# One core, XCiT attention into a gelu layer: hand-written issue order, fp32 batch-0 loads, transposed scores, two-bank gelu

## Chip, core and metric

The kernel runs on one core of a Trainium2 chip. The metric is device time in microseconds (us) of one execution. Before the change three timed runs gave 914.63, 913.44 and 914.12 us.

## What is computed

For each of 4 batches, q, k and v are 6080 x 256 in fp32. The attention is over channels: a 256 x 256 score matrix per batch, from columns normalised over the 6080 rows. Its result goes through a 256 to 2048 to 256 layer with gelu.

```python
qn = q / (np.linalg.norm(q, axis=1, keepdims=True) + 1e-06)
kn = k / (np.linalg.norm(k, axis=1, keepdims=True) + 1e-06)
s = kn.transpose(0, 2, 1) @ qn / tau
a = softmax(s, axis=-1)
x = (v @ a).reshape(24320, 256)
h = x @ w_in
out = gelu_tanh(h) @ w_out
```

Since v @ a @ w_in = v @ (a @ w_in), both kernels make aw = a @ w_in (256 x 2048, bf16) once per batch and then need for each row of v only hp = aw.T v and yp = gelu(hp).T w_out.

## The kernel before

A batch has two stages. **The Gram stage** (L81 to L115) walks 48 tiles of 128 rows (the last has 64). Each tile has two casting loads from the POOL queue, fp32 in HBM to bf16 in SBUF (L89, L90), squares on ScalarE (q, L92) and VectorE (k, L93), two Gram matmuls of 256 columns into G (L97), and for every second tile, after an addition on VectorE (L108), one matmul with a column of ones for the sums of squares (L109). Then come the norms and the softmax: a reciprocal on one partition (L118), square roots (L120, L121), a spread over 128 partitions by small fp32 matmuls (L124, L126), the scaled scores (L138), Exp (L139), four transposes on TensorE (L147) with copies (L153), and aw in 8 pieces of 512 columns (L161), evicted by ScalarE (L167).

**The block stage** (L170 to L215) walks 12 blocks of 512 rows of v (the last has 448). v is first cast to bf16 by one DRAM to DRAM transfer per batch (L82) and read by transposing DMAs on SP (L179). Each block has 32 matmuls hp of 512 columns (L187), 16 gelu on ScalarE of 128x512 each, from one PSUM bank (L192; the pool pH has 3), 64 matmuls yp of 256 columns (L199), four copies to SBUF (L203) and one store from the ScalarE queue (L207).

Nothing in the text fixes the order between the batches: a scheduler mixes the next batch's Gram tiles with the blocks as it sees fit. Each engine then runs its own list in order. Activation functions of different table sets need a table load (ACT_TABLE_LOAD) between them; the compiler places these.

Of the kernel before, what the change touches and what calls it, by code (L numbers as in the profile page):

```python
# [12 lines left out]


@with_exitstack
def kernel(
# [16 lines left out]
    assert isinstance(tau, (int, float)), "tau expected as a trace-time scalar"
    inv_tau2 = 1.0 / float(tau) ** 2

    def ntile_rows(n0):
        return min(128, N - n0)

    n_tiles = (N + 127) // 128  # L40
# [22 lines left out]
    nc.gpsimd.tensor_copy(ident_bf, ident)
    ones_col = const.tile([128, 1], BF16)
    nc.vector.memset(ones_col, 1.0)
    ones_row = const.tile([1, 128], FP32)
    nc.vector.memset(ones_row, 1.0)

    win_st = stage.tile([128, CHUNKS, D], FP32, tag="wst")
    nc.sync.dma_start(out=win_st, in_=moe_w_in.rearrange("(c p) d -> p c d", p=128))  # L70
    win_bf = const.tile([128, CHUNKS, D], BF16)
    nc.scalar.activation(win_bf, win_st, AF.Copy)  # L72

    wout_st = stage.tile([128, FC, 256], FP32, tag="wst")
# [2 lines left out]
    nc.scalar.activation(wout_bf, wout_st, AF.Copy)

    v_bf = dram.tile([B * N, C], BF16)

    for b in range(B):  # L81
        nc.gpsimd.dma_start(out=v_bf[b * N : (b + 1) * N, :], in_=v[b])  # L82
        G = pG.tile([128, CHUNKS, 512], FP32, tag="G")
        ss = pM.tile([1, 512], FP32, tag="m")
        for it in range(n_tiles):
            n0 = it * 128
            rows = ntile_rows(n0)
            qk = qkp.tile([128, 2, 256], BF16, tag="qk")
            nc.gpsimd.dma_start(out=qk[:rows, 0, :], in_=q[b, n0 : n0 + rows, :])  # L89
            nc.gpsimd.dma_start(out=qk[:rows, 1, :], in_=k[b, n0 : n0 + rows, :])  # L90
            sq = sqp.tile([128, 512], BF16, tag="sq")
            nc.scalar.activation(sq[:rows, 0:256], qk[:rows, 0, :], AF.Square)  # L92
            nc.vector.tensor_mul(sq[:rows, 256:512], qk[:rows, 1, :],  # L93
                                 qk[:rows, 1, :])
            first, last = it == 0, it == n_tiles - 1
            for ci in range(CHUNKS):
                nc.tensor.matmul(  # L97
                    G[:, ci, 0:256],
                    lhsT=qk[:rows, 1, ci * 128 : ci * 128 + 128],
                    rhs=qk[:rows, 0, :],  # L100
                    start=first,
                    stop=last,
                )
            if it % 2 == 0 and not last:
                sq_prev = sq
            else:
                if it % 2 == 1:
                    nc.vector.tensor_add(sq_prev[:rows], sq_prev[:rows], sq[:rows])  # L108
                nc.tensor.matmul(  # L109
                    ss,  # L110
                    lhsT=ones_col,
                    rhs=sq_prev,
                    start=it <= 1,
                    stop=last,
                )  # L115

        inv = smx.tile([1, 512], FP32, tag="inv")
        nc.vector.reciprocal(inv, ss)  # L118
        rrow = smx.tile([1, 512], FP32, tag="rrow")
        nc.scalar.activation(rrow[:, 0:256], inv[:, 0:256], AF.Sqrt)  # L120
        nc.scalar.activation(rrow[:, 256:512], inv[:, 256:512], AF.Sqrt,  # L121
                             scale=inv_tau2)
        M = pM.tile([128, 512], FP32, tag="m")
        nc.tensor.matmul(M[:, 0:256], lhsT=ones_row, rhs=rrow[0:1, 0:256])  # L124
        for ci in range(CHUNKS):
            nc.tensor.matmul(M[:, 256 + ci : 257 + ci],  # L126
                             lhsT=rrow[0:1, 256 + ci * 128 : 384 + ci * 128],
                             rhs=ident[0:1, 0:1], is_transpose=True)
        rqk = smx.tile([128, 258], FP32, tag="rqk")
        nc.vector.tensor_copy(rqk, M[:, 0:258])  # L130
        rk_col = rqk[:, 256:258]

        e_bf = smx.tile([128, 2, 256], BF16, tag="ebf")
        rsum = smx.tile([128, 2], FP32, tag="rsum")
        rsinv = smx.tile([128, 2], FP32, tag="rsinv")
        for ci in range(CHUNKS):
            S = smx.tile([128, 256], FP32, tag="S")
            nc.vector.tensor_mul(S, G[:, ci, 0:256], rqk[:, 0:256])  # L138
            nc.scalar.activation(e_bf[:, ci, :], S, AF.Exp,  # L139
                                 scale=rk_col[:, ci : ci + 1],  # L140
                                 accum_out=rsum[:, ci : ci + 1])
        nc.vector.reciprocal(rsinv, rsum)

        eTp = pG.tile([128, 4, 128], BF16, tag="G")
        for ci in range(CHUNKS):
            for jc in range(CHUNKS):
                nc.tensor.matmul(eTp[:, ci * 2 + jc, :],  # L147
                                 lhsT=e_bf[:, ci, jc * 128 : jc * 128 + 128],
                                 rhs=ident_bf, is_transpose=True)
        eT = smx.tile([128, 2, 256], BF16, tag="eT")  # L150
        for jc in range(CHUNKS):
            for ci in range(CHUNKS):
                nc.vector.tensor_copy(eT[:, jc, ci * 128 : ci * 128 + 128],  # L153
                                      eTp[:, ci * 2 + jc, :])

        aw = awp.tile([128, CHUNKS, D], BF16, tag="aw")
        for ic in range(CHUNKS):
            for fs in range(D // 512):
                awps = pH.tile([128, 512], FP32, tag="h")
                for jc in range(CHUNKS):  # L160
# [6 lines left out]
                nc.scalar.activation(aw[:, ic, fs * 512 : fs * 512 + 512], awps,  # L167
                                     AF.Copy, scale=rsinv[:, ic : ic + 1])

        for blk in range(n_blocks):  # L170
# [5 lines left out]
            vT = vts.tile([128, CHUNKS, 512], BF16, tag="vT")
            r0v = b * N + t0
            for cc in range(CHUNKS):
                nc.sync.dma_start_transpose(  # L179
                    out=vT[:, cc, :cols],  # L180
                    in_=v_bf[r0v : r0v + cols, cc * 128 : cc * 128 + 128])

            gs = []
            for fc in range(FC):
                hp = pH.tile([128, 512], FP32, tag="h")
                for cc in range(CHUNKS):
                    nc.tensor.matmul(hp[:, :cols],  # L187
                                     lhsT=aw[:, cc, fc * 128 : fc * 128 + 128],
                                     rhs=vT[:, cc, :cols],
                                     start=cc == 0, stop=cc == CHUNKS - 1)  # L190
# [60 lines left out]
```

## Time and profile before

| what | value |
|---|---|
| timed runs | 913.44, 914.12 (median), 914.63 us |
| profiled execution, first to last instruction | 913.5 us |
| mean granted TensorE clock | 0.955 of 2.4 GHz |
| PE busy | 804.7 us (88%) |
| ACT busy | 503.3 us (55%) |
| DVE busy | 190.3 us (21%) |
| POOL busy | 206.5 us (23%) |

The profile gives no time of its own for the profiled execution beside its span of 913.5 us. PE is the matmul engine, PEld its weight loads, DVE VectorE, ACT ScalarE, POOL GpSimd, SP the sync engine that here issues DMAs. An engine that is called busy need not run at its peak, as matmuls are pipelined; so rates are taken from start to start.

### The profile page before, as it was taken

The numbers are of one execution on the slowest core, as the hardware profiler recorded it, in microseconds if no ns is written. First come the engines' busy times: TensorE is split into PE (matmuls) and PEld (weight loads), VectorE is DVE, ScalarE is ACT, GpSimd is POOL, SyncE is SP. The second block draws the span as 40 slices with busy tenths as digits, with TensorE's granted clock in tenths as the row PEclk, the third lists the DMA queues.
The fourth block names the chain that finished last, engine by engine and source line by source line (L and its number), as shares of the span: only waits on it lengthen the run. The fifth ranks groups of instructions, "written<-read, shape, count | busy, mean of one in ns | idle before, by whom it ended". The sixth has DMA issues, their size and how long they took to land. (4 is left out here: it accounts for less than half of the span.)

```text
span 913.5 us, 13551 instructions
## 1 busy us (share of the span) xinstructions
PE 804.7 (88%) x5136; PEld 498.9 (55%) x5184; DVE 190.3 (21%) x518; ACT 503.3 (55%) x1031; POOL 206.5 (23%) x395
## 2 busy tenths in 40 slices
PE   0537529999999979999999889999999889999998
PEld 0101206666666637575666546575757545766666
DVE  0224302121221322121212313121212210101101
ACT  0333616565656385656566485656565466465563
POOL 2649412221212232312121222312121000000000
PEclk9995659999999989999999989999999999999999
DMA  9999984353534444534444434534443102212111
GB/s 234 232 177 122 187 155 76 82 87 76 81 80 78 85 46 76 96 72 90 73 85 74 90 36 82 92 70 93 70 92 67 55 12 58 58 56 61 46 47 44
DMA packets 134624, 79.80 MB, mean 87 GB/s; under 512 B 58784, under 2 KB 133792, under 8 KB 133792
## 3 DMA queue, kind: packets, MB, share of 16 engines
q0 software_dynamic: 55360, 37.38, 30.3%
q1 hardware_dynamic: 54048, 16.66, 8.2%
q10 hardware_dynamic: 25152, 24.91, 7.9%
q8 instruction: 40, 0.66, 0.3%
q14 instruction: 24, 0.20, 0.1%
HBM read 78.91 MB, written 37.36 MB: 127 GB/s over the span
## 5 line engine op out<-in xcount | busy, mean ns | idle before, releaser
L192 ACT ACTIVATE g<-hp 128x512 bf16<-128x512 f32 (+1 forms) x768 | 384.3, 625 | 275.2 <-PE hp L187 274.7
L199 PE MATMUL yp<-wout_bf,g 128*128 128x256 bf16 (+1 forms) x3072 | 372.8, 273 | 0.1
L187 PE MATMUL hp<-vT,aw 128*128 128x512 bf16 (+1 forms) x1492 | 368.3, 377 | 3.7 <-ACT g L192 1.3
L199 PEld LDWEIGHTS <-g 128*128 128x128 bf16 (+1 forms) x3072 | 300.4, 98 | 68.8 <-issue 0.8
L187 PEld LDWEIGHTS <-aw 128*128 128x128 bf16 x1536 | 148.7, 97 | 159.9 <-issue 35.9
L89 POOL DMA_DIRECT2D qk<-in_q_dram x192 | 111.0, 578 | 449.0 <-ACT g L192 360.9
L97 PE MATMUL G<-qk 128*128 128x256 bf16 (+1 forms) x384 | 79.2, 309 | 65.6 <-DMA qk<-in_k_dram 64.7
L203 DVE COPY ysb<-yp 128x256 f32<-128x256 f32 x192 | 81.2, 423 | 257.3 <-PE yp L199 257.1
L90 POOL DMA_DIRECT2D qk<-in_k_dram x192 | 112.6, 587 | 43.2 <-DMA v_bf<-in_v_dram 39.1
L92 ACT ACTIVATE sq<-qk 128x256 bf16<-128x256 bf16 x192 | 77.0, 455 | 76.9 <-DMA qk<-in_q_dram 54.9
L93 DVE TENSOR_TENSOR sq<-qk 128x256 bf16<-128x256 bf16 x192 | 54.9, 289 | 309.1 <-DMA qk<-in_k_dram 270.5
L97 PEld LDWEIGHTS <-qk 128*128 128x128 bf16 (+1 forms) x384 | 30.5, 101 | 118.3 <-DMA qk<-in_k_dram 94.1
L108 DVE TENSOR_TENSOR sq<-sq 128x512 bf16<-128x512 bf16 x96 | 40.7, 424 | 142.3 <-ACT sq L92 137.7
L109 PE MATMUL ss<-sq,ones_col 128*1 128x512 bf16 x96 | 41.8, 448 | 11.7 <-DVE sq L108 9.9
L167 ACT ACTIVATE aw<-awps,rsinv 128x512 bf16<-128x512 f32 x32 | 19.4, 695 | 9.7 <-PE awps L161 9.7
L161 PE MATMUL awps<-win_bf,eT 128*128 128x512 bf16 x60 | 20.5, 468 | 2.9 <-DVE eT L153 2.9
L124 PE MATMUL M<-rrow,ones_row 1*128 1x256 f32 x8 | 4.9, 710 | 19.7 <-ACT rrow L120 19.7
L109 PEld LDWEIGHTS <-ones_col 128*1 128x1 bf16 x96 | 7.7, 81 | 25.1 <-issue 24.7
L72 ACT ACTIVATE win_bf<-win_st 128x4096 bf16<-128x4096 f32 x1 | 3.6, 3618 | 20.9 <-DMA win_st<-in_moe_w_in_dram 20.9
L118 DVE RECIPROCAL inv<-ss 1x512 f32<-1x512 f32 x4 | 13.4, 3346 | 3.5 <-PE ss L109 3.5
L124 PEld LDWEIGHTS M<-rrow,ones_row 1*128 1x128 f32 x8 | 2.0, 306 | 21.2 <-ACT rrow L120 21.2
L161 PEld LDWEIGHTS <-eT 128*128 128x128 bf16 x64 | 7.1, 117 | 11.3 <-issue 5.5
(27 smaller groups left out, 47.7 us busy)
## 6 DMA issues: line engine op xcount, KB each, us to landing
out_dram<-ysb ACTq DMA_DIRECT2D x44, 512.0 KB, 2.9
v_bf<-in_v_dram POOLq DMA_DIRECT2D x4, 3040.0 KB, 20.8
qk<-in_q_dram POOLq DMA_DIRECT2D x188, 64.0 KB, 2.6
qk<-in_k_dram POOLq DMA_DIRECT2D x188, 64.0 KB, 2.6
win_st<-in_moe_w_in_dram SPq DMA_DIRECT2D x1, 2048.0 KB, 22.2
wout_st<-in_moe_w_out_dram SPq DMA_DIRECT2D x1, 2048.0 KB, 13.6
vT<-v_bf SPq DMA_TRANSPOSE x96, 2.7
out_dram<-ysb ACTq DMA_DIRECT2D x4, 384.0 KB, 2.5
```

The costliest lines, as they stand in the source:

```text
L89: nc.gpsimd.dma_start(out=qk[:rows, 0, :], in_=q[b, n0 : n0 + rows, :])
L90: nc.gpsimd.dma_start(out=qk[:rows, 1, :], in_=k[b, n0 : n0 + rows, :])
L92: nc.scalar.activation(sq[:rows, 0:256], qk[:rows, 0, :], AF.Square)
L93: nc.vector.tensor_mul(sq[:rows, 256:512], qk[:rows, 1, :], qk[:rows, 1, :])
L97: nc.tensor.matmul(G[:, ci, 0:256], lhsT=qk[:rows, 1, ci * 128 : ci * 128 + 128], rhs=qk[:rows, 0, :], start=first, stop=last,)
L108: nc.vector.tensor_add(sq_prev[:rows], sq_prev[:rows], sq[:rows])
L109: nc.tensor.matmul(ss, lhsT=ones_col, rhs=sq_prev, start=it <= 1, stop=last,)
L161: nc.tensor.matmul(awps, lhsT=eT[:, jc, ic * 128 : ic * 128 + 128], rhs=win_bf[:, jc, fs * 512 : fs * 512 + 512], start=jc == 0, stop=jc = ...
L187: nc.tensor.matmul(hp[:, :cols], lhsT=aw[:, cc, fc * 128 : fc * 128 + 128], rhs=vT[:, cc, :cols], start=cc == 0, stop=cc == CHUNKS - 1)
L192: nc.scalar.activation(g[:, :cols], hp[:, :cols], AF.Gelu_apprx_tanh)
L199: nc.tensor.matmul(yp[:r, 0:256], lhsT=gs[fc][:, s * 128 : s * 128 + r], rhs=wout_bf[:, fc, :], start=fc == 0, stop=fc == FC - 1)
L203: nc.vector.tensor_copy(ysb[:r, s, :], yp[:r, 0:256])
```

## The change

The new kernel turns the scheduler off (`manual_schedule`): each engine gets its instructions in the order of the text, and generators interleave the next batch's attention with the blocks, one step behind each pair of hp tiles.

- Batch 0: q and k come in fp32 by 20 HWDGE loads from SP (9 chunks of 2 to 6 tiles, four fp32 buffers), are cast on DVE and squared on ACT chunk by chunk; the sums of squares are a 128 x 512 matmul per tile with a square of ones, so that the sums stand on all partitions. The weights are loaded after q and k and cast by DVE and POOL. v of batch 0 is cast in four pieces.
- Batches 1 to 3: casting loads from POOL of 6 tiles each; squares and an fp32 running sum on DVE; one fp32 matmul with ones at the end.
- The scores are made transposed (lhsT = q, rhs = k), so the four transposes with their copies go; the row sums of the softmax come from four small matmuls (rs). The norms come from Ln and Exp in place of reciprocal and Sqrt. aw is evicted by DVE in place of ACT.
- gelu takes 128 x 1024 from two banks, 8 per block; yp of a block is put behind the hp of the next one, 8 matmuls at a time; two yp tiles share a bank and a copy of 128x512; stores go from SP.

```diff
-    qkp = ctx.enter_context(tc.tile_pool(name="qkp", bufs=6))
+    stage = ctx.enter_context(tc.tile_pool(name="stage", bufs=4))
+    qkp = ctx.enter_context(tc.tile_pool(name="qkp", bufs=4))
...
+    pA = ctx.enter_context(tc.tile_pool(name="pA", bufs=2, space=bass.MemoryType.PSUM))
+    pH = ctx.enter_context(tc.tile_pool(name="pH", bufs=2, space=bass.MemoryType.PSUM))
     pY = ctx.enter_context(tc.tile_pool(name="pY", bufs=2, space=bass.MemoryType.PSUM))
+    ctx.enter_context(tc.manual_schedule())
...
+    def softmax_steps(b, G, sums, aw):
+        SS = sums()
+        yield
...
+            nc.vector.scalar_tensor_tensor(
+                out=junk, in0=SS[:, jc * 128 : jc * 128 + 128], scalar=1.0, in1=ident,
+                op0=ALU.mult, op1=ALU.mult, accum_out=ssc[:, jc : jc + 1])
+        nc.scalar.activation(r[:, 0:256], SS[:, 256:512], AF.Ln, bias=tiny_b)
+        nc.scalar.activation(r[:, 256:258], ssc, AF.Ln, bias=tiny_b)
+        yield
+        nc.scalar.activation(r, r, AF.Exp, scale=0.5)
+        nc.scalar.activation(r, r, AF.Ln, bias=eps_b)
+        nc.scalar.activation(r, r, AF.Exp, scale=-1.0)
+        yield
...
+            nc.scalar.activation(eT[:, jc, :], S[:, jc, :], AF.Exp,
+                                 scale=r[:, 256 + jc : 257 + jc])
+        yield
+        rs = pA.tile([128, 512], FP32, tag="a", name="rs")
...
+        nc.vector.reciprocal(rsinv, rs[:, 0:2])
+        yield
+        for fs in range(D // 512):
+            for ic in range(2):
...
+                nc.vector.tensor_scalar_mul(
+                    aw[:, ic, fs * 512 : fs * 512 + 512], ps, rsinv[:, ic : ic + 1])
+                yield
...
+    first_chunks = chunks_of([2, 5, 6, 6, 6, 6, 6, 6, 4])
...
+            nc.vector.tensor_copy(qkb[:rows, lo:hi], st[:rows, lo:hi])
+            nc.scalar.activation(sqb[:rows, lo:hi], st[:rows, lo:hi], AF.Square)
...
+        if n == 6:
+            nc.gpsimd.tensor_copy(gate[:, 0:1], st[0:1, 0, 0, 0:1])
+            nc.gpsimd.dma_start(out=v_bf[0:1024, :], in_=v[0, 0:1024, :])
...
+    for half in range(2):
+        nc.gpsimd.tensor_copy(wout_bf[:, half * 8 : half * 8 + 8, :], wout_st[half])
...
+    V_CH = [(1024, 2688), (2688, 4384), (4384, N)]
+    for lo, hi in V_CH:
+        nc.gpsimd.dma_start(out=v_bf[lo:hi, :], in_=v[0, lo:hi, :])
...
+    def attention_steps(b, aw_next):
...
+        for n in range(3):
+            load(n)
+        for _ in range(8):
+            yield
...
+                gram(G, loaded[n], s, rows, first, last)
+                flat = loaded[n][:rows, s].rearrange("p a b -> p (a b)")
...
+                    nc.vector.tensor_mul(sq[:rows], flat, flat)
+                    nc.vector.tensor_add(acc[:rows], acc[:rows], sq[:rows])
+                seen += 1
+                yield
+                if seen % 2:
+                    yield
+        def sums():
+            SS = pA.tile([128, 512], FP32, tag="a", name="SS")
+            nc.tensor.matmul(SS, lhsT=ones_f, rhs=acc)
+            return SS
+        yield from softmax_steps(b, G, sums, aw_next)
...
+            for i in range(NP):
+                hp = pH.tile([128, 2, 512], FP32, tag="h", name="hp")
...
+                nc.scalar.activation(g[:, 2 * i : 2 * i + 2, :cols], hp[:, :, :cols],
+                                     AF.Gelu_apprx_tanh)
+                if nb == 0:
+                    next(steps, None)
+                if before is not None:
+                    h = i % 2
+                    y_part(before, i // 2, h * NP, h * NP + NP)
+                next(fill, None)
```

What a generator yields takes one step of the block loop. `attention_steps` gives 8 empty steps, 72 steps for 48 Gram tiles, and 13 for the softmax and aw, of the 96 steps that 12 blocks have; so the softmax of batch b+1 falls into block 10 of batch b, and its aw into blocks 10 and 11.

**ScalarE at the softmax of a batch.** The rows of before, for a later batch; the names are the program's tiles (rrow the norms, e_bf the exponentials, g the gelu output):

```order
L120 ACT_TABLE_LOAD
L120 ACTIVATE rrow<-inv 1x256
L121 ACTIVATE rrow<-inv 1x256
L92 ACTIVATE sq<-qk 128x256 x2
L139 ACT_TABLE_LOAD
L139 ACTIVATE e_bf,rsum<-S,rqk 128x256 x2
L167 ACTIVATE aw<-awps,rsinv 128x512 x8
L192 ACT_TABLE_LOAD
L192 ACTIVATE g<-hp 128x512 x16
```

The rows of the change in block 10 of batch 0, behind a table load, the two Ln of the sums (L142, L143), a table load and one gelu:

```order
L145 ACT_TABLE_LOAD
L145 ACTIVATE r<-r 128x258
L146 ACT_TABLE_LOAD
L146 ACTIVATE r<-r,eps_b 128x258
L147 ACT_TABLE_LOAD
L147 ACTIVATE r<-r 128x258
L375 ACT_TABLE_LOAD
L375 ACTIVATE g<-hp 128x1024
L155 ACT_TABLE_LOAD
L155 ACTIVATE eT<-S,r 128x256 x2
L375 ACT_TABLE_LOAD
L375 ACTIVATE g<-hp 128x1024 x4
```

Three table loads per batch have become eight (five for batch 0, whose softmax has no gelu between its steps), and gelu stand between the steps of the softmax.

**TensorE one step later in the same block**, where the row sums rs stand between a yp group and the next hp:

```order
L319 LDWEIGHTS g
L319 MATMUL yp<-wout_bf,g 128x256
L161 LDWEIGHTS eT [waits Activation_49]
L161 MATMUL rs<-ones_bf,eT 128x1 [waits DVE_49]
L161 LDWEIGHTS eT [waits Activation_49]
L161 MATMUL rs<-ones_bf,eT 128x1
```

Before, the transposes of e_bf waited for Exp at this point; now rs does, and all hp and yp of the blocks stand behind it in the list.

**POOL at the start.** Before:

```order
L82 DMA v_bf<-in_v_dram 128x12160
masks.py:199 ISA
masks.py:199 AFFINE_SELECT ident<-ident 128x128
L89 DMA qk<-in_q_dram 128x256
L63 CAST ident_bf<-ident 128x128
L90 DMA qk<-in_k_dram 128x256
```

With the change (wst are the fp32 weights):

```order
L208 COPY gate<-st 1x1 [waits DMAHW6_49]
L209 DMA v_bf<-in_v_dram 16x16384
L247 CAST win_bf<-wst 128x2x512 [waits DMAHW4_49]
L247 CAST win_bf<-wst 128x2x512 [waits DMAHW5_49]
L250 CAST wout_bf<-wst 128x2048 [waits DMAHW6_49]
L250 CAST wout_bf<-wst 128x2048 [waits DMAHW7_49]
L258 DMA v_bf<-in_v_dram 32x13312
L258 DMA v_bf<-in_v_dram 32x13568 x2
L86 DMA qkb<-in_q_dram 128x5x256 [waits DVE_49,PE_49]
```

The rest of v and the first q and k of batch 1 are now issued behind the casts of the weights, which wait for loads that stand behind all of batch 0's q and k.

## Rows read from the trace of the kernel before

**Rows 1.** The page, part 1: busy us (share of the span), instructions.
```profile
PE 804.7 (88%) x5136; PEld 498.9 (55%) x5184; DVE 190.3 (21%) x518; ACT 503.3 (55%) x1031; POOL 206.5 (23%) x395
```

**Rows 2.** Stretches: length, busy by engine (instructions), granted clock, DMA share, GB/s.
```profile
0.00:23.00 23.00, 0.00 (x0) 0.00 (x0) 0.21 (x2) 1.36 (x2) 5.30 (x15) 1.00 0.93 234
70.00:100.00 30.00, 20.11 (x58) 4.49 (x59) 15.99 (x41) 13.33 (x31) 27.29 (x52) 0.50 1.05 128
...
724.00:742.00 18.00, 10.37 (x39) 4.30 (x39) 5.31 (x9) 11.93 (x21) 0.00 (x0) 0.81 0.02 6
...
756.00:896.00 140.00, 139.43 (x942) 92.26 (x949) 16.57 (x39) 79.23 (x158) 0.00 (x0) 1.00 0.19 53
...
120.00:124.00 4.00, 0.00 (x0) 0.00 (x0) 0.00 (x0) 0.00 (x0) 0.00 (x0) 0.50 1.10 237
```

**Rows 3.** Timeline, start of the blocks: start us, length, engine, line, count [idle <-releaser].
```profile
109.33 0.59 PE L187 MATMUL hp<-vT,aw 128*128 128x512 bf16 x2
...
130.74 0.53 POOL L90 DMA_DIRECT2D qk<-in_k_dram  x1 [13.69 <-DMA v_bf<-in_v_dram]
...
131.18 1.25 PE L97 MATMUL G<-qk 128*128 128x256 bf16 x4 [19.73 <-DMA qk<-in_k_dram]
```

**Rows 4.** Chain that ended last, blocks of batches 2 and 3: start us, length, what.
```profile
573.00 1.73 PE hp L187 x8
...
762.21 6.44 PE yp L199 x59
...
776.37 6.44 PE yp L199 x59
```

**Rows 5.** Groups by line and shape: busy us, mean ns of one | idle before, releaser.
```profile
L192 ACT ACTIVATE g<-hp 128x512 bf16<-128x512 f32 x704 | 355.3, 630 | 251.1 <-PE hp L187 250.7 <-issue 0.2
L108 DVE TENSOR_TENSOR sq<-sq 128x512 bf16<-128x512 bf16 x92 | 39.0, 424 | 128.7 <-ACT sq L92 124.2
L192 ACT ACTIVATE g<-hp 128x448 bf16<-128x448 f32 x64 | 29.0, 576 | 24.0 <-PE hp L187 24.0
L139 ACT ACT_TABLE_LOAD x4 | 5.1, 1283 | 0.1
L124 PE MATMUL M<-rrow,ones_row 1*128 1x256 f32 x8 | 4.9, 710 | 19.7 <-ACT rrow L120 19.7
L139 ACT ACTIVATE e_bf<-S,rqk 128x256 bf16<-128x256 f32 x8 | 4.0, 500 | 1.7 <-DVE S L138 1.6
L72 ACT ACTIVATE win_bf<-win_st 128x4096 bf16<-128x4096 f32 x1 | 3.6, 3618 | 20.9 <-DMA win_st<-in_moe_w_in_dram 20.9
L138 DVE TENSOR_TENSOR S<-G,rqk 128x256 f32<-128x256 f32 x8 | 3.0, 420 | 0.1
L120 ACT ACTIVATE rrow<-inv 1x256 f32<-1x256 f32 x4 | 1.7, 415 | 2.6 <-DVE inv L118 2.6
L63 POOL CAST ident_bf<-ident 128x128 bf16<-128x128 f32 x1 | 0.3, 303 | 0.0
```

**Rows 6.** The page, part 3: DMA queue, packets, MB, share of 16 engines' span.
```profile
q0 software_dynamic: 55360, 37.38, 30.3%
...
q10 hardware_dynamic: 25152, 24.91, 7.9%
```

**Rows 7.** Timeline, ScalarE at the last table load.
```profile
734.42 4.74 ACT L167 ACTIVATE aw<-awps,rsinv 128x512 bf16<-128x512 f32 x8 [2.27 <-PE awps L161]
...
739.18 1.28 ACT L192 ACT_TABLE_LOAD   x1
...
740.47 5.99 ACT L192 ACTIVATE g<-hp 128x512 bf16<-128x512 f32 x12
```

**Rows 8.** Timeline, end of the program.
```profile
903.27 6.72 PE L199 MATMUL yp<-wout_bf,g 128*128 128x256 bf16 x59
...
910.48 0.49 ACTq L214 DMA_DIRECT2D out_dram<-ysb  x1
```

More of the change, by code (lines that the diff above doesn't have):

```diff
@@ L30 @@
     D = moe_w_in.shape[1]
-    assert C == 256 and D % 128 == 0
-    CHUNKS = C // 128
+    assert C == 256 and D == 2048
+    assert isinstance(tau, (int, float)), "tau expected as a trace-time scalar"
+    inv_tau = 1.0 / float(tau)
     FC = D // 128
[L34 to L40, printed above, removed]
+    NP = FC // 2
     BLK = 512
     n_blocks = (N + BLK - 1) // BLK
+    S_ALL = N // 128
@@ L60, with slots_of @@
+    def slots_of(chunk):
+        _, size, rem = chunk
+        return [(s, 128) for s in range(size)] + ([(size, REM)] if rem else [])
+    first_chunks = chunks_of([2, 5, 6, 6, 6, 6, 6, 6, 4])
+    views0 = qk_views(0)
+    staged = []
+    for ch in first_chunks[:4]:
+        st = stage.tile([128, SMAX, 2, 256], FP32, tag="st", name="st")
+        load_chunk(nc.sync, st, views0, ch)
+        staged.append(st)
     ident = const.tile([128, 128], FP32)
     make_identity(nc, ident)
-    ident_bf = const.tile([128, 128], BF16)
@@ L63 @@
[L63 to L74, printed above, removed]
@@ L75 @@
-    nc.sync.dma_start(out=wout_st, in_=moe_w_out.rearrange("(t p) d -> p t d", p=128))
-    wout_bf = const.tile([128, FC, 256], BF16)
[L77 to L96, printed above, removed]
-                nc.tensor.matmul(
[L98 to L160, printed above, removed]
@@ new lines @@
+    steps = softmax_steps(0, G, lambda: SS, aw)
+    next(steps)
+    next(steps)
+    for half in range(2):
+        nc.vector.tensor_copy(win_bf[:, :, half * 1024 : half * 1024 + 512],
+                              win_st[half][:, :, 0:512])
+        nc.gpsimd.tensor_copy(win_bf[:, :, half * 1024 + 512 : half * 1024 + 1024],
+                              win_st[half][:, :, 512:1024])
+    for half in range(2):
+        nc.gpsimd.tensor_copy(wout_bf[:, half * 8 : half * 8 + 8, :], wout_st[half])
@@ L170 @@
+    before = None
+    for b in range(B):
+        if b + 1 < B:
+            aw_next = awp.tile([128, 2, D], BF16, tag="aw", name="aw")
+            fill = attention_steps(b + 1, aw_next)
+        else:
+            aw_next, fill = None, iter(())
         for blk in range(n_blocks):
+            nb = b * n_blocks + blk
             t0 = blk * BLK
             cols = min(BLK, N - t0)
-            subs = [min(128, cols - s * 128) for s in range((cols + 127) // 128)]
-            nfull = sum(1 for r in subs if r == 128)
@@ L176 @@
[L176 to L190, printed above, removed]
-                g = gp.tile([128, 512], BF16, tag="g")
-                nc.scalar.activation(g[:, :cols], hp[:, :cols], AF.Gelu_apprx_tanh)
-                gs.append(g)
@@ L219 @@
+            before = now
+        for _ in fill:
+            pass
+        aw = aw_next
+    for s in range(4):
+        y_part(before, s, 0, FC)
 _INS = ['q', 'k', 'v', 'tau', 'moe_w_in', 'moe_w_out']
```

239 lines of the change are left out of this document (205 added, 34 removed).

## The prediction

> **What bounds the kernel now.** I read the page first: PE is busy for 88% of the span and no other engine for more than 55% [rows 1]. That is an average, so I went to the windows next. From 756 to 896 us PE has work for 139.4 of 140 us at a granted clock of 1.00 (2.4 GHz): there only fewer or faster matmuls help. In the first 23 us PE does nothing, from 70 to 100 it has work for 20 of 30 us at a clock of 0.50 (1.2 GHz), and from 724 to 742, at the last softmax, for 10.4 of 18 us at 0.81 [rows 2]. The timeline of the start gives the third reading: the first hp stands at 109.3 us, but behind a few of them a Gram matmul of batch 1 waits for q and k behind the cast of v, and PE is idle for 19.7 us to 131.2 us [rows 3]. So before the blocks run 131 us are gone. The chain of waits gives the pace of the blocks after that: from one yp group of 59 to the next 776.37 - 762.21 = 14.16 us. A yp takes 6.44 / 59 = 0.1092 us, an undisturbed hp 1.73 / 8 = 0.2163 us [rows 4]. 64 yp and 32 hp make 6.99 + 6.92 = 13.91 us; the other 0.25 us per block is hp waiting for gelu, of which ScalarE does 12 in 5.99 us, 0.50 us each, while the two hp of one take 0.43 [rows 7].
>
> **The blocks, new.** hp of 32 per block stay, but one gelu of 1024 now stands against 4 hp and 8 yp, 0.87 + 0.87 = 1.74 us. From 448 to 512 columns a gelu grows by 54 ns [rows 5], so 1024 columns take 0.63 + 512 x 0.054 / 64 = 1.06 us. That is under 1.74, so the 0.25 us go: 13.91 us per block, 13.05 us for a batch's last (448 columns). A batch is 11 x 13.91 + 13.05 = 166.1 us, four are **664.2**. If two banks don't stream as one, the gelu is two of 0.63 = 1.26 us, still under 1.74.
>
> To this come the Gram matmuls of batches 1 to 3, 3 x 96 x 0.109 = **31.4**; aw, 64 x 0.216 = 13.8, less the first four, which lie ahead of the first hp, **13.0**; and three fp32 sums of 512 columns, twice the 0.71 us of 256 [rows 5], **4.3**. The sums of squares in bf16 that PE did for these batches (144 tiles, one matmul of 512 for two) are gone: 72 x 0.22 = 16 us that this sum does not contain.
>
> Costed at nothing: DVE does in a block of about 14.8 us four squares (0.42 each, [rows 5]), four fp32 additions (at most twice that) and two copies of 512 (twice 0.42 each), under 7 us. POOL's loads are 16 large ones for 96; queue q0 held its engines for 30.3% of the span, 69 us per batch [rows 6], against 166 us. On SP the stores now stand behind the transposing loads, which are asked for two blocks ahead. If that cover fails, hp waits for vT or a Gram matmul for q and k.
>
> **The start.** Batch 0 now comes by 12.45 MB of fp32 in pieces of 1 KB, as the rows of the output store are. That queue (q10) moved 24.91 MB in 7.9% of 913.5 us, 72.2 us, so 345 GB/s [rows 6]: 36.1 us. With 3 us for the first issue and the last landing, and 2.3 us for the cast of v's first 1024 rows among it, q and k are there at 41.4 us. Bounds: the cast queue q0 took 30.3% x 913.5 x 16 / 55360 = 80 ns per packet and engine, by which 12160 pieces take 61 us; a read of 400 GB/s, which the first 23 us come near to when the casts are counted with their fp32 sources [rows 2], 31 us. I take the store's rate, as its pieces have this size and no cast. Then the last chunk is squared, 2048 elements at 3618 / 4096 ns [rows 5], 1.8 us, and four tiles take PE 1.7 us: 45 us. The softmax: two Ln (0.50, 0.42), three table loads at 1.28 = 3.85, Exp, Ln, Exp at 0.50, the scores 0.42 and two Exp 1.0 [rows 5], 7.7 us; the row sums, their reciprocal and the first two pieces of aw with their copies about 2. The first hp starts at **55**, between 50 and 80 by those bounds.
>
> Block 0 has no yp to fill its gaps: an aw piece goes through DVE before its hp, 3 waits of about 0.5, and PE starts at the lower clock. From 724 to 742 the mean of 0.81 means 18 x 0.19 / 0.5 = 6.8 us at 1.2 GHz [rows 2]; I take 4 us of work there at half speed, 2 us lost each time PE has rested long (0 to 3.4). Together **3.5**.
>
> The first Gram matmul of batch 1 stands behind block 0 and the first yp, at 55 + 13 + 1.7 = 69.7 us. Its data stand behind the casts on POOL: the second half of w_out lands 4.2 MB after q and k, at 53.6 us, its cast of 2048 takes 0.3 us (the row for 128 elements) to 4.8 us (16 times that) [rows 5], I take 3; then 2.6 MB of v and 0.7 MB of q and k (in bf16), 14 us at the 237 GB/s of 120 to 124 us or 26 at the 128 GB/s of 70 to 100 us [rows 2]; I take 16, near the first, whose stretch was a cast of v too. With 2 us for landing they are there at 74.6: a wait of 5 (0 to 20), and 2 for the clock, **7**.
>
> **The softmax inside the blocks.** This is the price of the new order. From the end of the gelu ahead of Ln to the end of the two last Exp, ScalarE has seven table loads at 1.283 = 9.0 us, two gelu 2.1 us, and Ln, Ln, three of 258 columns and two Exp, 0.50 + 0.42 + 1.5 + 1.0 = 3.4 us [rows 5]: 14.5 us. PE has until then what is left of the yp group, three steps of 1.74, and less 0.3 us that ScalarE lags: 4.9 us of work. Then rs waits for the exponentials, and all hp and yp stand behind it. PE waits 14.5 - 4.9 = 9.6 us, then 2 us for the clock: 11.6, three times, **34.8**. In the kernel before, ScalarE's table loads run without a gap: aw ends at 734.42 + 4.74 = 739.16, the load runs from 739.18 for 1.28 us and gelu starts at 740.47 [rows 7]; 1.283 us is the whole price.
>
> On this one rule speaks against the change. The Trainium skill (ScalarE: Activation LUTs, What ACT_TABLE_LOAD costs) gives a switch 1.28 us for the load and about 1.38 us for a drain, 2.66 us in all; by that the sum would be, as an estimate, 25 x 1.38 = about 35 us longer (25 switches on the path, seven per batch and four at the start). The trace agrees with the load and shows no drain [rows 7].
>
> **The end.** The last yp ends at 909.99 and the span at 913.5, behind a copy and a store issued at 910.48 [rows 8]: **3.5**, as before.
>
> **The sum** is 55 + 664.2 + 31.4 + 13.0 + 4.3 + 3.5 + 7 + 34.8 + 3.5 = 816.7 us, against the span of 913.5; the median of the runs is 0.6 us above that span, so 817 us. The 97 us are chiefly the start (131 to 55 with 7 more at the first Gram wait, 69), the 16 us of sums of squares and the 12 us of 48 blocks; the waits at the softmax stay about what they were.
>
> **The rivals.**
> - *The fp32 loads go at the cast queue's price per packet.* For it: most loads of the trace go by that queue, and a price per packet rather than per byte would carry over. Against: the store's queue has pieces of the same size and 345 GB/s. 61 for 36 us: 842.
> - *hp keeps its old pace.* For it: the 0.25 us may not be ScalarE's. Against: gelu at 0.50 us paces just that stage. 48 x 0.25: 829.
> - *A switch between tables costs twice its row*, as activations around it cannot overlap when every one is followed by a switch. For it: before, only three stand in a batch, apart from each other. Against: rows 7. Seven per batch and four at the start, (21 + 4) x 1.28 = 32: 849.
> - *The waits are covered.* No wait at the first Gram and no slow clock, 7 + 2 + 6 less: 802.
> - *Gram starves the blocks*, on the other side: PE takes its list in order, so each hp behind a Gram matmul waits for that tile's load, as at 131.18. It decides when queue q0 needs more for a batch's 9.3 MB than the 180 us that a batch now has; to be slower than before, 97 us more in three batches, it must need 212 us, 44 GB/s. Against: 237 GB/s in the stretch where it had the engines alone [rows 2]. 915 or more.
>
> **How the numbers follow.** Forecast 0.58 (800 to 835 by its bounds); loads 0.14; old pace 0.10; switches 0.08; covered 0.07; starving 0.03. The range 797 to 852 takes in all but the last and the forecast's own tails. A measurement here can tell 0.2%, about 2 us: faster 0.96, the same 0.01, slower 0.03.
>
> **What would show it.** Right: the first hp near 55 us; in the blocks one yp group and hp at 13.9 us without Gram; three waits of rs for ScalarE of some 8 to 10 us at L161; eight loads of 1.28 us per batch; a few us at the first G for q and k. Wrong: table loads with gaps of over 1 us behind them, gelu over 1.7 us, G waiting in every batch, or q and k not there by 50 us.

## The result and the profile after

| | before | after |
|---|---|---|
| median of 4 runs, us | 914.38 (913.44 to 916.49) | 819.95 (819.54 to 821.35) |
| ratio, 95% interval | | 0.8972 [0.8957, 0.8988] |
| profiled execution: its time, its span, us | span 913.5 | 820.13, 818.0 |
| mean granted TensorE clock | 0.955 | 0.973 |

The change takes 94.4 us off. The forecast was 817, 0.4% below the median, inside its range of 797 to 852. The row of the page that answers to [rows 1]:

```profile
PE 755.3 (92%) x5126; PEld 503.1 (62%) x5126; DVE 258.6 (32%) x461; ACT 461.9 (56%) x452; POOL 58.5 (7%) x81
```

PE is busy for 49 us less, and the span is 95 us shorter: about half of the gain is time in which PE was busy (fewer matmuls, and fewer of them at the lower clock), the other half time in which it stood idle. Of the 95.5 us, 53.9 lie ahead of the first Gram matmul of batch 1 and 41.6 behind it. POOL's instructions fall from 395 to 81; DVE has more to do and is still at a third.

**The start**, in the timeline, against [rows 3]; first PE, then DVE, then ScalarE:

```profile
42.24 0.60 PE L122 MATMUL G<-qkb 128*128 128x256 bf16 x2 [3.62 <-DVE qkb L194]
...
49.35 0.38 PE L199 MATMUL SS<-sqb,ones_bf 128*128 128x512 bf16 x1
58.85 0.19 PE L161 MATMUL rs<-ones_bf,eT 128*128 128x1 bf16 x1 [9.12 <-ACT eT L155]
...
61.21 0.61 PE L371 MATMUL hp<-vT,aw 128*128 128x512 bf16 x1
...
77.27 0.38 PE L122 MATMUL G<-qkb 128*128 128x256 bf16 x2
...
43.24 1.23 DVE L194 CAST qkb<-st 128x2048 bf16<-128x2048 f32 x1 [1.05 <-DMA st<-in_k_dram]
...
50.18 0.29 DVE L139 SCALAR_TENSOR_TENSOR junk<-SS,ident 128x128 f32<-128x128 f32 x1
...
77.08 0.69 DVE L292 TENSOR_TENSOR acc<-qkb 128x512 f32<-128x512 bf16 x1 [3.53 <-DMA qkb<-in_k_dram]
...
50.56 1.28 ACT L142 ACT_TABLE_LOAD   x1 [5.43 <-DVE junk L139]
51.86 0.47 ACT L142 ACTIVATE r<-SS,tiny_b 128x256 f32<-128x256 f32 x1
```

The last chunk of q and k is there at 43.24 us, when DVE begins to cast it. PE has rested for 3.62 us before the last but one and is through with both only at 49.7. The softmax then holds PE for 9.12 us, the first hp starts at 61.21 us (before: 109.33), and the first Gram matmul of batch 1 at 77.27 us (before: 131.18) without any wait in brackets: before, 19.73 us stood there. It was close: DVE, which squares the same chunk, had to wait for it until 77.08 us.

**Stretches** (length, busy us and instructions of PE, PEld, DVE, ACT, POOL, granted clock, DMA share, GB/s), against [rows 2]:

```profile
10.00:20.00 10.00, 7.32 (x32) 3.53 (x32) 3.56 (x3) 5.39 (x3) 0.00 (x0) 1.00 1.09 349
...
39.00:50.00 11.00, 7.12 (x30) 3.67 (x30) 3.14 (x3) 4.67 (x2) 2.07 (x2) 0.69 1.06 380
...
230.00:237.00 7.00, 6.79 (x31) 3.59 (x32) 0.92 (x2) 4.33 (x5) 0.00 (x0) 0.61 0.02 4
240.00:300.00 60.00, 60.00 (x418) 40.39 (x417) 19.57 (x35) 31.91 (x32) 1.65 (x2) 1.00 0.32 65
```

The fp32 loads run at 349 GB/s. In the blocks PE is busy without a gap at a clock of 1.00; at the end of batch 0's load, and behind the softmax at 230 us, part of the stretch goes at 1.2 GHz.

**The blocks**, in the chain that ended last, against [rows 4]; the same yp group one block apart:

```profile
700.84 0.87 PE yp L319 x8
...
714.73 0.87 PE yp L319 x8
```

That is 13.89 us, eight steps of 0.87 + 0.87. **The softmax of batch 1** in block 10, in the timeline of PE and then of ScalarE, against [rows 7]:

```profile
220.46 1.02 PE L371 MATMUL hp<-vT,aw 128*128 128x512 bf16 x4 [1.07 <-ACT g L375]
...
229.91 0.19 PE L161 MATMUL rs<-ones_bf,eT 128*128 128x1 bf16 x1 [7.55 <-ACT eT L155]
230.31 0.24 PE L161 MATMUL rs<-ones_bf,eT 128*128 128x1 bf16 x3 [0.21 <-ACT eT L155]
...
216.12 1.28 ACT L142 ACT_TABLE_LOAD   x1
...
227.01 1.02 ACT L375 ACTIVATE g<-hp 128x1024 bf16<-128x1024 f32 x1
228.05 1.28 ACT L155 ACT_TABLE_LOAD   x1
229.35 0.91 ACT L155 ACTIVATE eT<-S,r 128x256 bf16<-128x256 f32 x2
```

ScalarE works from 216.12 to 230.26 us without a pause; PE waits for it 1.07 + 7.55 + 0.21 = 8.83 us. In the waits of the whole span (us, times, longest) the row of rs holds 9.1 of batch 0 and three times the above:

```profile
PE rs L161 <- ACT eT L155: 32.6, 8, 9.1
```

**Groups by line and shape**, against [rows 5]:

```profile
L375 ACT ACTIVATE g<-hp 128x1024 bf16<-128x1024 f32 x352 | 360.1, 1024 | 286.7 <-PE hp L371 286.6
...
L375 ACT ACT_TABLE_LOAD x10 | 12.8, 1283 | 0.2
```

**The end**, in the timeline, against [rows 8]:

```profile
805.75 8.14 PE L319 MATMUL yp<-wout_bf,g 128*128 128x256 bf16 x72
...
814.39 0.93 SPq L341 DMA_DIRECT2D out_dram<-ysb  x2
```

A gelu of 1024 takes 1.02 us and waits only for hp; the last yp ends at 813.89, the span at 818.0.

### The profile page after: what moved, and what is told of

Its sections match the earlier page's. It is cut to its first block, busy times and chain, and to the rows that moved or that the text cites. A ratio compares the mean times of both kernels' runs of the same rounds, so it can differ in the third digit from the quotient of the medians.

```text
span 818.0 us, 11879 instructions
## 1 busy us (share of the span) xinstructions
PE 755.3 (92%) x5126; PEld 503.1 (62%) x5126; DVE 258.6 (32%) x461; ACT 461.9 (56%) x452; POOL 58.5 (7%) x81
## 4 chain that ended last, share of the span: by engine, by line
PE 89%; ACT 6%; DMA 4%; DVE 1%; SPq 0%; issue 0%; DVEq 0%; ACTq 0%
PE yp L319 41%; PE hp L371 40%; PE G L122 4%; DMA st<-in_k_dram 4%; PE ps L173 2%; ACT sqb L195 1%; ACT g L375 1%; ACT L147 1%; ACT L146 1%; ACT L145 1%; ACT L155 0%; ACT L375 0%; ACT eT L155 0%; PE SS L199 0%; DVE aw L178 0%; PE SS L304 0%
## 5 line engine op out<-in xcount | busy, mean ns | idle before, releaser
L375 ACT ACTIVATE g<-hp 128x1024 bf16<-128x1024 f32 (+1 forms) x384 | 389.4, 1015 | 316.8 <-PE hp L371 316.7
L371 PE MATMUL hp<-vT,aw 128*128 128x512 bf16 (+1 forms) x1536 | 396.0, 380 | 5.6 <-ACT g L375 3.5
L319 PE MATMUL yp<-wout_bf,g 128*128 128x256 bf16 (+1 forms) x3072 | 399.4, 274 | 0.0
L333 DVE COPY ysb<-yp 128x512 f32<-128x512 f32 x92 | 63.6, 692 | 410.5 <-PE yp L319 410.5
L296 DVE TENSOR_TENSOR acc<-acc,sq 128x512 f32<-128x512 f32 (+1 forms) x141 | 97.6, 692 | 4.8
L122 PE MATMUL G<-qkb 128*128 128x256 bf16 (+1 forms) x384 | 76.8, 283 | 15.7 <-DVE qkb L194 15.7
L122 PEld LDWEIGHTS <-qkb 128*128 128x128 bf16 (+1 forms) x384 | 37.5, 100 | 36.9 <-DVE qkb L194 19.0
L295 DVE TENSOR_TENSOR sq<-qkb 128x512 bf16<-128x512 bf16 (+1 forms) x141 | 58.8, 417 | 0.0
L178 DVE TENSOR_SCALAR aw<-ps,rsinv 128x512 bf16<-128x512 f32 x32 | 24.0, 749 | 39.3 <-PE ps L173 39.2
L195 ACT ACTIVATE sqb<-st 128x3072 bf16<-128x3072 f32 (+4 forms) x10 | 22.4, 2250 | 15.9 <-DMA st<-in_k_dram 15.8
L375 ACT ACT_TABLE_LOAD x10 | 12.8, 1283 | 0.2
```

The lines of the kernel that those rows point to most:

```text
L122: nc.tensor.matmul(G[:, jc, :], lhsT=qk[:rows, s, 0, jc * 128 : jc * 128 + 128], rhs=qk[:rows, s, 1, :], start=first and jc == 0, stop=las ...
L178: nc.vector.tensor_scalar_mul(aw[:, ic, fs * 512 : fs * 512 + 512], ps, rsinv[:, ic : ic + 1])
L195: nc.scalar.activation(sqb[:rows, lo:hi], st[:rows, lo:hi], AF.Square)
L295: nc.vector.tensor_mul(sq[:rows], flat, flat)
L296: nc.vector.tensor_add(acc[:rows], acc[:rows], sq[:rows])
L319: nc.tensor.matmul(yp[:rows, s % 2, :], lhsT=g[:, fc, s * 128 : s * 128 + rows], rhs=wout_bf[:, fc, :], start=fc == 0, stop=fc == FC - 1)
```

## The experiments

Each differs from the changed kernel (819.95 us) by the edit shown; e9, e8 and e10 combine edits of the runs that they name. The theories, by the letters of the quoted texts: for the waits in the blocks, A, ScalarE's chain in the softmax sets them, against B, the place of rs in PE's list does; for the pace of the blocks, A, the new order gives it, against C, the two-bank gelu; for the start, D, size and order of the loads, against E, the fp32 queue itself; and F, what the first hp gains reaches the end, against G, the first Gram matmul swallows it.

### e1: two table loads less in each softmax

```diff
-        yield
-        nc.scalar.activation(r, r, AF.Exp, scale=0.5)
-        nc.scalar.activation(r, r, AF.Ln, bias=eps_b)
-        nc.scalar.activation(r, r, AF.Exp, scale=-1.0)
+        yield
+        nc.scalar.activation(r, r, AF.Exp, scale=-0.5)
         yield
```

> It takes Ln and one Exp out of the norms: r = exp(-0.5 ln(ss)) in place of 1 / (exp(0.5 ln(ss)) + 1e-06), so it leaves out the 1e-06 added to the norms; the places of gelu and of the steps stay. Theory A (ScalarE's serial work up to the two last Exp sets the wait of rs): two table loads of 1.28, one Ln of 0.51 and one Exp of 0.42, 3.5 us, go from each of the three waits and from the start: 820 - 14 = 806, and the wait of rs inside the blocks falls from 7.6 us to about 4. Theory B (rs stands too early in TensorE's list, or the data come late for another reason): 820, the waits as they were.

Measured: 810.33 us (809.56 to 810.83), ratio 0.8848 [0.8830, 0.8866]. Waits of PE (us, times, longest), then its timeline:

```profile
PE rs L159 <- ACT eT L153: 18.4, 8, 5.6
...
PE G L122 <- DMA qkb<-in_k_dram: 3.5, 1, 3.5
```

```profile
76.42 0.38 PE L122 MATMUL G<-qkb 128*128 128x256 bf16 x2 [3.45 <-DMA qkb<-in_k_dram]
...
227.17 0.18 PE L159 MATMUL rs<-ones_bf,eT 128*128 128x1 bf16 x1 [3.99 <-ACT eT L153]
```

The wait in a block falls from 7.55 to 3.99, by 3.56 us; two loads (2 x 1.283), one Ln (0.51) and one Exp (0.42) are 3.50. So ScalarE's chain lies on the path and a load costs its row, no more: A. In the start the same 3.5 us are gained (9.12 to 5.6), but the first Gram matmul now waits 3.45 us for batch 1's data and starts only 0.85 us earlier. That makes 3 x 3.56 + 0.85 = 11.5 us and not the 14 of A; between the profiled spans (818.0 and 807.4) it is 10.6, by the medians 9.6.

### e2: rs three steps later in PE's list

```diff
+        for _ in range(3 if b else 0):
+            yield
         rs = pA.tile([128, 512], FP32, tag="a", name="rs")
```

> The row sums rs of batches 1 to 3 are issued three block steps (12 hp and 24 yp matmuls) later; ScalarE's list is the same. Theory A: the wait goes over to hp, which needs the gelu behind the table loads: hp waits some 5 to 8 us per batch at L371, rs nothing; at most 2 us per batch are won, 814 to 820. Theory B (the place of rs holds the blocks up): the wait of about 8 us and the clock's 2 go, three times: 790.

Measured: 816.21 us (815.04 to 817.24), 0.8913 [0.8893, 0.8933]. Timeline of PE, then a row of its waits:

```profile
228.62 1.86 PE L373 MATMUL hp<-vT,aw 128*128 128x512 bf16 x4 [5.72 <-ACT g L377]
...
233.17 1.02 PE L373 MATMUL hp<-vT,aw 128*128 128x512 bf16 x4 [0.98 <-ACT g L377]
```

```profile
PE hp L373 <- ACT g L377: 23.7, 10, 5.7
```

In the blocks rs waits no longer, but hp does, for the gelu that stand behind the same ScalarE work: 23.7 us of wait of hp in place of 23.3 at rs and 3.5 at hp. So 3.1 us of wait are saved, and 3.7 us by the medians, where B had promised 30. A holds, B falls.

### e3: gelu of one bank, order unchanged

```diff
-                hp = pH.tile([128, 2, 512], FP32, tag="h", name="hp")
                 for j in range(2):
                     fc = 2 * i + j
+                    hp = pH.tile([128, 512], FP32, tag="h", name="hp")
...
+                    nc.scalar.activation(g[:, fc, :cols], hp[:, :cols],
+                                         AF.Gelu_apprx_tanh)
```

(pH with four tiles of one bank, so as many banks as before.)

> gelu takes 128x512 from one bank again, 16 per block, with four one-bank tiles in place of two of two banks; the order of matmuls is that of the change. Theory A (the order, yp between the hp, takes the pressure off ScalarE, whose 16 x 0.5 = 8 us then fit easily into 13.9): a block without Gram stays at 13.9 us, 818 to 823 in all. Theory C (the wide gelu buys the pace): the 0.25 us per block of before come back, 832.

Measured: 820.48 us (818.37 to 821.62), 0.8957 [0.8930, 0.8983], the same as the changed kernel. Its group:

```profile
L375 ACT ACTIVATE g<-hp 128x512 bf16<-128x512 f32 x704 | 381.9, 595 | 264.3 <-PE hp L371 264.1
```

Two gelu of 0.595 us are 1.19, still under the 1.74 us of a step, and 264 us of ScalarE's idle time ahead of them is waiting for hp. A block of the last batch takes 13.89 us as in the changed kernel. The two-bank gelu is not what gives the pace: C falls.

### e4: yp behind its own block's hp, in one piece

```diff
-                if before is not None:
-                    h = i % 2
-                    y_part(before, i // 2, h * NP, h * NP + NP)
                 next(fill, None)
+            for s in range(4):
+                y_part(now, s, 0, FC)
```

> The yp of a block come behind its own hp, in one piece, in place of between the hp of the next block; gelu stays wide. Theory A: then 8 gelu of 1.02 us run against 32 hp of 6.9 us; a block without Gram needs 0.86 + 6 x 1.02 + 0.86 + 6.99 = 14.8 us, 0.95 more, where Gram tiles fill the gap (0.9 us per block) nothing; at the softmax TensorE has no yp to do while ScalarE is busy, some 3 us more per batch: 820 + 12 + 9 = 841 (830 to 850). Theory C (the wide gelu alone makes the pace): 820.

Measured: 862.38 us (861.26 to 862.69), 0.9415 [0.9395, 0.9435]. A block of the last batch in PE's timeline:

```profile
713.16 7.15 PE L319 MATMUL yp<-wout_bf,g 128*128 128x256 bf16 x64
720.15 1.89 PE L371 MATMUL hp<-vT,aw 128*128 128x512 bf16 x8
722.35 1.94 PE L371 MATMUL hp<-vT,aw 128*128 128x512 bf16 x8 [0.31 <-ACT g L375]
724.48 1.94 PE L371 MATMUL hp<-vT,aw 128*128 128x512 bf16 x8 [0.20 <-ACT g L375]
...
728.39 3.88 PE L319 MATMUL yp<-wout_bf,g 128*128 128x256 bf16 x34
```

Now two gelu stand against eight hp: eight hp take 2.13 to 2.20 us from start to start where PE alone needs 1.73, and the block 728.39 - 713.16 = 15.23 us. The direction is that of A, the size was missed by 21 us. I had let the Gram tiles fill the gap; but a block with six Gram tiles takes 15.6 us (15.2 in the changed kernel), and at each softmax hp waits 3.28 us for gelu where it waited 1.07, since all of hp stands ahead of all of yp. 12 x 1.34 + 36 x 0.4 + 3 x 2.2 = 37 of the 42 us; the rest I can't place. The 15.23 us are also more than the 14.16 of before [rows 4], whose yp stood nearly in one piece too (59 of 64) and whose gelu took one bank: in that order the wide gelu, with its two tiles, brings nothing.

### e5: batch 0 by casting loads of the same size

```diff
-        st = stage.tile([128, SMAX, 2, 256], FP32, tag="st", name="st")
-        load_chunk(nc.sync, st, views0, ch)
+        st = qkp.tile([128, SMAX, 2, 256], BF16, tag="qk", name="qkb")
+        load_chunk(nc.gpsimd, st, views0, ch)
...
-            nc.vector.tensor_copy(qkb[:rows, lo:hi], st[:rows, lo:hi])
```

(The weights are issued from POOL too, to stay behind q and k.)

> Batch 0's q and k come by casting loads from POOL in the same nine chunks, straight to bf16, with no cast on DVE; the weights are loaded from the same queue behind them. Theory D (loads go by the bytes read, some 349 GB/s of fp32 as in the change between 10 and 30 us): q and k are there at about 40 us as before, first hp at 58 to 63, 816 to 822 in all. Theory E (they go by the packet: in the change queue q0 took 25.9% x 818 x 16 / 38096 = 89 ns per packet and engine, and here 24320 packets of 512 B are written): q and k need up to 135 us, first hp 60 to 95 us later, 880 to 915.

Measured: 819.02 us (818.25 to 819.42), 0.8949 [0.8920, 0.8977], the same as the changed kernel. A stretch of its start, and in the timeline the first hp and the first Gram matmul of batch 1:

```profile
10.00:20.00 10.00, 7.50 (x25) 3.34 (x25) 0.00 (x0) 5.10 (x2) 3.31 (x4) 1.00 1.43 192
```

```profile
54.59 0.61 PE L369 MATMUL hp<-vT,aw 128*128 128x512 bf16 x1
...
75.01 0.58 PE L122 MATMUL G<-qkb 128*128 128x256 bf16 x2 [4.43 <-DMA qkb<-in_k_dram]
```

Counted in bf16 as [rows 2] are, 192 GB/s stand for 384 of fp32. The casting loads feed the Gram matmuls as well as the fp32 queue does, and the first hp comes 6.6 us earlier (no cast on DVE stands between, and v's cast stands in one queue behind the loads; e6, which moves v's cast alone, gains 3.8); then 4.43 us go in waiting for batch 1. Theory E falls: from 10 to 40 us the casting queue passed 10657 packets, one per 45 ns on each of 16 engines, where E had put 89 ns and 24320 packets. So neither the fp32 format nor its queue brings the start its gain.

The loads are larger (2 to 6 tiles for 1) and stand in another order (q and k ahead of the weights and of v). No experiment parts those two, but the trace of before shows a price of each. For the order, three loads of k wait for casts of v, 17.06, 8.40 and 13.69 us, until 23.33, 60.82 and 130.74 us, and a Gram matmul starts on PE within 0.5 us behind each:

```profile
POOL qk L90 <- DMA v_bf<-in_v_dram: 39.1, 3, 17.1
```

For the size, from 70 to 96 us that queue carried nothing but single tiles of q and k and moved 122 GB/s, with POOL busy issuing for 27.29 of the 30 us up to 100 [rows 2]; e5's large loads moved 192 to 217 GB/s between 10 and 40 us, with POOL busy for 3.3 to 5.0 of 10 us.

### e6: v's first rows behind the last chunk

```diff
-        if n == 6:
+        if n == 8:
```

> The cast of v's first 1024 rows is issued behind batch 0's last q and k chunk in place of the seventh. Theory F (the start is bounded by q and k): they land 2 to 3 us sooner, TensorE does not rest for 3.6 us ahead of the last two chunks, the first hp comes 3 to 4 us sooner: 816. Theory G (the first Gram matmul of batch 1 at 77 us takes back what the start gains, as its data stand behind the casts of v): first hp sooner, a wait of some 3 us at L122, 819 to 821.

Measured: 821.57 us (821.10 to 821.98), 0.8979 [0.8955, 0.9003].

```profile
57.42 0.61 PE L371 MATMUL hp<-vT,aw 128*128 128x512 bf16 x1
...
77.45 0.58 PE L122 MATMUL G<-qkb 128*128 128x256 bf16 x2 [4.91 <-DMA qkb<-in_k_dram]
```

The cast of v among q and k costs the first hp 3.8 us (the last chunk is there 1.4 us sooner, at 41.85, and PE, which has hardly rested, has no backlog at the lower clock). It costs the end nothing: the 3.8 us come back as a wait of 4.91 at the Gram matmul, which starts at 77.45 as against 77.27. G holds, F falls.

### e9: e1, and batch 1's first chunk ahead of v's casts

```diff
-    for lo, hi in V_CH:
+    for lo, hi in V_CH[:1]:
         nc.gpsimd.dma_start(out=v_bf[lo:hi, :], in_=v[0, lo:hi, :])
...
             load(n)
+            if b == 1 and n == 0:
+                for lo, hi in V_CH[1:]:
+                    nc.gpsimd.dma_start(out=v_bf[lo:hi, :], in_=v[0, lo:hi, :])
```

> The version with two table loads less per softmax (which leaves out the 1e-06 added to the norms), and the first q and k chunk of batch 1 is issued ahead of the second and third of v's casts, 3.4 MB of fp32 read. Theory G: the wait of 3.5 us at the first Gram matmul goes, 810 - 3.5 = 806. If the data are late for another reason: 810.

Measured: 805.56 us (804.68 to 807.65), 0.8808 [0.8781, 0.8834].

```profile
74.99 0.38 PE L122 MATMUL G<-qkb 128*128 128x256 bf16 x2
```

The wait of e1 is gone, and the median falls by 4.8 us (805.56 and 810.33), to what G forecast. In the two profiled executions the Gram matmul starts only 1.4 us earlier, and the spans differ by 1.9 us (805.5 and 807.4). The two profiles stand at opposite ends of their runs (e9's is the slowest of its four, e1's the fastest): in e9's, PE rested for 3.98 us ahead of the last but one chunk (e1: 3.37), did more of its tiles at the lower clock, and reached the first hp at 58.68 us, 1.7 us later than in e1.

### e7: sums of squares of batches 1 to 3 on PE

```diff
-                    nc.vector.tensor_mul(sq[:rows], flat, flat)
-                    nc.vector.tensor_add(acc[:rows], acc[:rows], sq[:rows])
+                nc.vector.tensor_mul(sq[:rows], flat, flat)
+                nc.tensor.matmul(SS, lhsT=ones_bf[:rows, :], rhs=sq[:rows],
+                                 start=first, stop=last)
```

> The sums of squares of batches 1 to 3 are made on TensorE as in batch 0, one matmul of 512 columns with ones per tile, in place of the fp32 running sum on DVE with one fp32 matmul at the end. TensorE bounds the blocks, so 144 x 0.216 = 31 us come in and 3 x 1.0 go: 848. If the blocks had slack: under 835.

Measured: 884.47 us (884.29 to 884.65), 0.9667 [0.9641, 0.9692]. A piece of the chain that ended last, and a row of PE's waits:

```profile
153.36 0.07 DVE ysb L329
153.43 0.54 issue
153.97 0.42 DVE sq L292
154.39 0.04 issue
154.44 0.38 PE SS L293
```

```profile
PE SS L293 <- DVE sq L292: 32.2, 36, 0.9
```

144 matmuls at 0.216 are 31 us, as expected; the other half I had not seen. SS stands in PE's list right behind its square on DVE, and where a copy of ysb stands ahead of that square, PE waits 0.9 us: 36 times, 32.2 us. 31 + 32 less the three fp32 sums (3) are 60 of the 64.5 us. The sums of squares are off PE's path only with the addition on DVE as well.

### e8 and e10: what was learnt, put together

e8 is e9 with all of ScalarE's softmax work in one step (three table loads per batch for eight), Ln's first table loaded ahead of the weights, and e6's place for v's first cast; two yields ahead of rs keep it at the step where it stood:

```diff
         nc.scalar.activation(r[:, 256:258], ssc, AF.Ln, bias=tiny_b)
-        yield
-        nc.scalar.activation(r, r, AF.Exp, scale=0.5)
-        nc.scalar.activation(r, r, AF.Ln, bias=eps_b)
-        nc.scalar.activation(r, r, AF.Exp, scale=-1.0)
-        yield
+        nc.scalar.activation(r, r, AF.Exp, scale=-0.5)
...
+        yield
+        yield
         rs = pA.tile([128, 512], FP32, tag="a", name="rs")
...
-        if n == 6:
+        if n == 8:
...
+    nc.scalar.activation(gate[0:1, 4:5], eps_b[0:1, 0:1], AF.Ln)
```

> What the runs point to, together: the norms by exp(-0.5 ln(ss)), which leaves out the 1e-06 added to them; all of the softmax's ScalarE work in one block step, so that three table loads per batch remain; one Ln on a constant behind the last square, so that the first table load is not on the path; v's first 1024 rows cast behind batch 0's last chunk; batch 1's first chunk ahead of the second and third of v's casts. Theory A: from the gelu ahead of Ln to the next gelu's end 3 x 1.28 + 0.47 + 0.29 + 0.42 + 0.5 + 0.9 + 1.02 = 7.5 us, of which TensorE has 3.2 us of work: a wait of 4.3 for 8.6 us and less of the slow clock, 5 to 6 us saved per batch, 16 in all; the start as far as the first Gram matmul at 70 in place of 77 us: 820 - 23 = 797. If the waits come from elsewhere: 805.

Measured: 798.94 us (798.78 to 799.50), 0.8722 [0.8701, 0.8743]. A row of PE's waits, and its timeline:

```profile
PE hp L374 <- ACT g L378: 12.9, 4, 4.2
```

```profile
217.35 1.87 PE L374 MATMUL hp<-vT,aw 128*128 128x512 bf16 x4 [4.20 <-ACT g L378]
...
51.49 0.18 PE L159 MATMUL rs<-ones_bf,eT 128*128 128x1 bf16 x1 [4.29 <-ACT eT L151]
55.24 1.92 PE L374 MATMUL hp<-vT,aw 128*128 128x512 bf16 x4 [1.81 <-DMA vT<-v_bf]
```

One wait of 4.20 us per softmax in place of 8.83, as the expectation said. In the start rs waits 4.29 us where e1 had 5.6: the table load that was taken out of the path, 1.3 us. What stands next there is v: the first hp now waits 1.81 us for its transposed rows, and the first Gram matmul starts at 71.03 us (70 expected). e10 is e8 with e5's loads and the cast of v behind the seventh chunk:

> The same with batch 0 loaded by the casting queue (and the cast of v's first rows behind the seventh chunk). Theory D (the size of the loads counts, not the queue): the same 797 within 3 us.

Measured: 796.68 us (794.98 to 797.90), 0.8694 [0.8673, 0.8715], the fastest version here; beside e8, whose interval overlaps, no clear difference. Both leave out what e1 leaves out.

## Why the prediction was right, and where its terms were off

| term of the sum, us | predicted | measured |
|---|---|---|
| first hp | 55 | 61.2 |
| first hp to first Gram matmul, with its wait and clock | 13 + 1.7 + 7 = 21.7 | 77.27 - 61.21 = 16.1 |
| a block without Gram | 13.91 | 13.89 |
| three fp32 sums | 4.3 | 3 x 1.01 = 3.0 |
| softmax in three batches | 34.8 | 3 x (8.8 + 2.7) = 34.6 |
| end | 3.5 | 4.1 |

**The blocks** are confirmed by step, pace and cause: 13.89 us, gelu 1.02 against 1.06 predicted, no wait for gelu. The rival of the old pace falls, and e3 and e4 say why: the order puts 1.74 us of matmuls against each step's gelu, one or two, and that alone is enough. One sentence of the prediction was too strong: from 756 to 896 us PE had been counted busy for 139.4 of 140 us, "there only fewer or faster matmuls help", and yet the same matmuls in another order take 0.27 us less per block. The busy share did not show those waits; the rate from start to start did.

**The softmax** is confirmed by mechanism and size. ScalarE takes 230.26 - 216.10 = 14.2 us (predicted 14.5); PE has 5.3 us of work meanwhile (4.9) and waits 8.83 (9.6). From 230 to 237 the clock's mean of 0.61 means 7 x 0.39 / 0.5 = 5.5 us at 1.2 GHz, 2.7 us lost (2). The wait of 1.07 at hp ahead of rs had not been named; it is part of the same chain. Of the rival of the double switch nothing is left: each group of loads in the profile has 1283 ns, the next activation starts 0.02 us behind, and e1's saving of 3.56 us counts two loads at just that. The rival that the waits are covered falls too: only the wait at the first Gram matmul stayed out, for the reason below. By the rule of the Trainium skill (ScalarE: Activation LUTs, What ACT_TABLE_LOAD costs), 2.66 us per switch with its drain, e1 would have gained 2 x 2.66 + 0.93 = about 6.2 us per softmax, as an estimate; the run decides for 1.28.

**The start** failed by 6.2 us, in two steps. The first is that "the last chunk is squared ..., and four tiles take PE 1.7 us: 45 us" came out as 49.7. The chunk came at 43.2 for 41.4; but the step took PE as free and at full clock. PE had rested for 3.62 us ahead of the last but one chunk (in e6, where v's cast doesn't load beside it, that wait is 0.95 us, and the first hp 3.8 us earlier). It then had 10 tiles to do for 4, most of them at 1.2 GHz: 0.85 us per tile where 0.43 is usual. The second is that the "three table loads" on the path were four, as the prediction's own rival had counted: 9.4 us from 49.85 to 59.2 for 7.7. The first load stands behind DVE's two sums of the diagonal, though Ln (L142) reads only SS, which PE had finished at 49.7. The list of ScalarE's instructions in the compiled program shows the reason, for batch 0 and then for a later batch:

```
L142 ACT_TABLE_LOAD [waits DVE_49]
L142 ACTIVATE r<-SS,tiny_b 128x256 [waits PE_49]
...
L142 ACT_TABLE_LOAD
L142 ACTIVATE r<-SS,tiny_b 128x256 [waits DVE_49]
```

In batch 0, Ln has two waits, and the one for DVE's sums stands on the load ahead of it. In e8, where that table is loaded early, Ln itself still waits for those sums (it starts at 48.05 us), so only the load has left the path.

**The first Gram wait** failed in the other direction: 5 and 2 for the clock were predicted, none came, and block 0 lost 4.8 us to gaps and the lower clock (16.1 less 9.5 for its matmuls and 1.7 for a step) for 3.5. The data came 2.5 us later than the forecast 74.6: DVE has them at 77.08, and e1, e5 and e6 wait for them until 75.0 to 77.5. PE came 0.2 us after them, and so did not wait. That the two errors cancel is mechanism: batch 1's data bound what stands ahead of them, and an earlier first hp only lengthens the wait, as e6 shows (3.8 us off the start, nothing off the end). That PE and the data met within 0.2 us is luck.

**A wrong reason.** The prediction costed the fp32 loads by the store's rate, and the 345 GB/s were right (349 measured). The rival "fp32 at the cast queue's price per packet" falls by that. But the 80 ns per packet was no price of that queue either: in e5 it carried the same tiles, in large pieces and at the head, as fast, at 45 ns per packet and engine. That the fp32 format matters was not said in so many words, but the sum read as if it did; e5 shows that it does not.

**Sums of squares.** The 16 us that the sum leaves out are right in sign; e7 shows that a matmul per tile would have cost 31 us and its place in the list as much again.

The differences above add up to about -1 us, the span is 1.3 us above the sum of 816.7: some 2.5 us of 818 are not placed. The starving Gram stage did not come: outside the start no Gram matmul waits. What the transposed scores and the eviction of aw by DVE bring by themselves is not shown, as no run takes them back alone.

## What to carry to other kernels

When the text sets the order, look for the longest chain on a side engine that the main engine meets in its list, and shorten that: moving the waiting instruction (e2) hands most of the wait to the next one, while fewer table loads (e1, e8) take it away. Put against each activation at least as much matmul work as it lasts and the pace is the matmuls', as here at either width of gelu. A gain ahead of a point that waits for data ends there (e6, and e1 until e9): move the data's issue first.
